# Clustered attention and two MLPs on one core: warming products read keys, the exponential's table is loaded early, the planner gets other durations, the second batch's values are read later

## The chip, the cores and the metric

The kernel runs on one core of a Trainium2 chip. The metric is the device time of one execution in microseconds (us). Engines are named as the profile names them: PE (TensorE, matrix products; PEld is its weight load), DVE (VectorE), ACT (ScalarE), POOL (GpSimd), SP (SyncE, which here issues every DMA).

## What is computed

Attention in which a query sees only the keys of its own cluster, then two MLPs in fp32 accuracy:

```
q_assign = argmax(q_n . c_n);  k_assign = argmax(k_n . c_n)      # 16 clusters per head, cosine
scores = where(q_assign == k_assign, q k^T / 8, -1e9)            # 2 batches, 8 heads, 768 x 768, head 64
attn = softmax(scores);  x = attn @ v                            # then (batch*seq, heads*64) = 1536 x 512
h = max(x @ w_in, 0);  x = (h * h) @ w_out                       # 512 -> 2048 -> 512
x = (sigmoid(x @ w_gate) * (x @ w_val)) @ w_out2                 # 512 -> 1536 -> 512
```

The MLP weights come as 64-bit floats and are turned into a high and a low fp32 part on the chip.

## The kernel before

**Attention.** Each of 16 heads has six score tiles of 128 queries by 768 keys, 96 in all, numbered n = 6 * head + i; tiles 2p and 2p+1 are pair p. For a tile PE makes the scores (`t_qk`) into one of two or three PSUM tiles `s`, DVE the negated maximum `nm` (`t_max`), ACT the exponential (`t_exp`) in place with a sum. Then ACT copies an fp16 high half into `hl` (`t_hi`) and DVE the low half (`t_lo`, L869). With both tiles of the pair done, one DMA transpose on SP makes `pt` from `hl` (`t_turn`, L878), and PE multiplies it with the values' halves `vh`, `vl` into `po` (`t_pv`). Pairs listed in `by_pe` go another way: the exponential is written to SBUF (`e`), PE transposes it (`tb`, L906), ACT or DVE copy it out (`ptf`), and the product with raw fp32 values follows. DVE scales `po` into `xp` (L961).

**A head's operands.** Raw queries and keys of two heads lie in one tile (`raw`, six buffers, loads on SP). Queries are scaled by 0.125 in place. For each head after the first, four tables T1, T2 (queries) and M1, M2 (keys) are built: a copy (`T<-raw`, `M<-raw`: ACT, DVE or POOL), a second copy (`T<-T`, `M<-M`: ACT, DVE, POOL, or a DMA), a subtraction (`T<-raw,T`, `M<-raw,M`: DVE or POOL), and rows of the one-hot assignment `oh` by DMA. The one-hot rows come from ten DVE steps on dots with the centroids (`as`), one set per four heads.

**The start** is written out by hand: 10 and 11 products that only keep PE at work (`keep_busy`), the dots, the first assignment, and `rt`, a square root on ACT.

**Order.** All else is put in order when the kernel is built, by `Planner`: a list scheduler with a duration per engine for each task (`{"a": 790, "p": 850}` lets ACT or POOL do it), a priority (mostly the tile's number less an offset out of `PLAN`), a time after which a result is seen (`SETTLE`), and counts of free buffers. DVE and POOL tasks marked `vp` are not put side by side. Each engine then runs its own list strictly in order. Weight conversions of the MLPs and the first third of the first MLP (`g`, `y` for 512 tokens) are put between the attention's work; the rest follows.

The second batch's values (`load_v`, six loads on SP, `vr`) may be issued from `v_later`, 50 us on the planner's clock.

```
def keep_busy(r, n):
    for _ in range(n):
        mm(busy[:, : r.shape[-1]], ident, r, True, True)
```

## Time and profile before

| | us |
|---|---|
| median of 3 runs (833.34 to 834.13) | 834.05 |
| profiled execution | 831.97 |
| its span | 830.2 |
| PE busy | 766.0 (92%) |
| DVE busy | 547.9 (66%) |
| ACT busy | 447.8 (54%) |
| POOL busy | 266.4 (32%) |

The shares are means over two different stages: up to about 360 us attention and MLP work run side by side, after it PE works through the MLPs alone. A busy share of the whole span therefore says little on what a change in the first stage is worth; the rows further down are taken by stretch. The span runs from the first instruction's start to the last one's end; the execution's own time has 1.8 us more.

### The profile page before, as it was taken

To read this page: it belongs to the slowest core of one execution; us is meant where nothing else is said; L and a number is where in the kernel's file an instruction comes from. 1 tells how busy PE (TensorE), PEld (TensorE's weight loads), DVE (VectorE), ACT (ScalarE), POOL (GpSimd) and SP (SyncE) were. 2 spreads that over 40 slices of the span, in tenths; PEclk is the share of its full clock that TensorE was granted. 3 is DMA by queue.
4 is the path that set the end of the run, shared out by engine and by line. 5 is a ranking of instruction groups with operands and counts; after the bars stand their busy time and mean duration, and the time that the engine had idled before them with its cause. 6 is when DMAs were issued, how large, how long until landed. Compare 5 with 4: busy or idle time off the path is not lost.

```text
span 830.2 us, 12473 instructions
## 1 busy us (share of the span) xinstructions
PE 766.0 (92%) x4721; PEld 633.7 (76%) x4721; DVE 547.9 (66%) x865; ACT 447.8 (54%) x800; POOL 266.4 (32%) x322
## 2 busy tenths in 40 slices
PE   8778687789888979799999999999999999999998
PEld 4468576668776868688888888888888888888886
DVE  5689888989999998868376776924333427933300
ACT  2989767778887675758564563422212225612300
POOL 3955646486555323334041322111111113100000
PEclk9889789999999989999999999999999999999999
DMA  6599997966889788732232322411211222100101
GB/s 201 137 191 211 181 191 158 214 130 137 165 207 212 180 194 185 268 102 95 83 127 76 102 80 98 135 68 54 98 51 51 76 78 102 51 24 27 39 26 38
DMA packets 143420, 100.56 MB, mean 121 GB/s; under 512 B 124128, under 2 KB 124128, under 8 KB 143360
## 3 DMA queue, kind: packets, MB, share of 16 engines
q1 hardware_dynamic: 143360, 99.76, 47.4%
q8 instruction: 37, 0.61, 0.3%
q14 instruction: 23, 0.19, 0.1%
HBM read 62.10 MB, written 3.15 MB: 79 GB/s over the span
## 4 chain that ended last, share of the span: by engine, by line
PE 68%; DVE 11%; DMA 8%; ACT 6%; issue 4%; POOL 1%; SPq 1%; DVEq 0%; POOLq 0%; ACTq 0%
PE y L310 14%; PE o L310 12%; PE pv L310 12%; PE pg L310 12%; PE g L310 11%; DMA pt<-hl 5%; DVE nm L839 3%; PE po L310 3%; PE s L310 3%; DMA wo0r<-in_moe_w_out_dram 2%; DVE hl L869 2%; ACT s L854 2%; ACT hl L317 2%; DMA raw<-in_k_dram 1%; DVE M L319 1%
## 5 line engine op out<-in xcount | busy, mean ns | idle before, releaser
L310 PE MATMUL s<-M,T 128*128 128x384 f32 x360 | 88.5, 375 | 28.2 <-DVE hl L869 14.2
L839 DVE TENSOR_REDUCE nm<-s 128x1 f32<-128x768 f32 x96 | 90.3, 950 | 10.6 <-PE s L310 9.9
L310 PEld LDWEIGHTS s<-M,T 128*128 128x128 f32 x360 | 65.2, 204 | 38.8 <-issue 14.1
L1442 DVE SCALAR_TENSOR_TENSOR gv<-th,pv 128x512 f32<-128x512 f32 x36 | 24.6, 687 | 98.2 <-PE pv L310 98.2
L1435 ACT ACTIVATE th<-pg 128x512 f32<-128x512 f32 x36 | 21.5, 598 | 123.9 <-PE pg L310 120.1
L854 ACT ACTIVATE s<-s,nm 128x768 f32<-128x768 f32 x78 | 68.1, 873 | 24.1 <-DVE nm L839 23.7
L869 DVE TENSOR_TENSOR hl<-s,hl 128x768 f16<-128x768 f32 x78 | 73.7, 948 | 4.0 <-ACT hl L317 3.6
L310 PEld LDWEIGHTS <-pt 128*128 128x128 f16 x1404 | 49.4, 104 | 24.0 <-DMA pt<-hl 13.8
L310 PE MATMUL po<-vh,pt 128*128 128x64 f16 x936 | 53.9, 202 | 13.8 <-DMA pt<-hl 9.1
L317 ACT ACTIVATE hl<-s 128x768 f16<-128x768 f32 x78 | 63.3, 811 | 1.9
L310 PE MATMUL po<-vl,pt 128*128 128x64 f16 x468 | 51.0, 202 | 0.0
L1471 ACT ACTIVATE ot<-o 128x512 f32<-128x512 f32 x12 | 7.2, 599 | 81.0 <-PE o L310 81.0
L1369 ACT ACTIVATE r<-g 128x512 f32<-128x512 f32 x48 | 28.7, 598 | 26.5 <-PE g L310 26.4
L1180 POOL TENSOR_SCALAR wgm<-wgm 128x512 f32<-128x512 f32 x12 | 7.7, 643 | 104.5 <-ACT wgm L1172 92.9
L1411 DVE TENSOR_TENSOR yf<-yf,y 128x512 f32<-128x512 f32 x36 | 24.7, 685 | 17.9 <-PE y L310 17.5
L776 POOL TENSOR_TENSOR T<-raw,T 64x768 fp32r<-64x768 f32 x15 | 29.3, 1954 | 4.1 <-ACT T L317 3.1
L782 POOL TENSOR_TENSOR M<-raw,M 64x768 fp32r<-64x768 f32 x15 | 28.3, 1887 | 1.4 <-DVE M L319 0.5
L1375 ACT ACTIVATE g<-r 128x512 f32<-128x512 f32 x47 | 28.3, 601 | 0.9
L1298 DVE TENSOR_TENSOR gs_0l<-gv,gs_0h 128x512 fp32r<-128x512 f32 x3 | 2.1, 690 | 39.3 <-ACT gs_0h L317 39.3
L1180 POOL TENSOR_SCALAR wi1m<-wi1m 128x512 f32<-128x512 f32 x16 | 10.4, 652 | 52.6 <-ACT wi1m L1172 45.6
L310 PEld LDWEIGHTS po<-vr,ptf 128*128 128x128 f32 x216 | 25.6, 192 | 0.2 <-DVE xp L961 0.2
L310 PE MATMUL po<-vr,ptf 128*128 128x64 f32 x216 | 25.6, 272 | 0.0
(583 smaller groups left out, 2359.5 us busy)
## 6 DMA issues: line engine op xcount, KB each, us to landing
wi0r<-in_moe_w_in_dram SPq DMA_DIRECT2D x16, 512.0 KB, 4.3
wo0r<-in_moe_w_out_dram SPq DMA_DIRECT2D x16, 512.0 KB, 4.0
wi1r<-in_moe_w_in_dram SPq DMA_DIRECT2D x16, 512.0 KB, 3.4
wo1r<-in_moe_w_out_dram SPq DMA_DIRECT2D x16, 512.0 KB, 3.3
wgr<-in_moe_w_gate_dram SPq DMA_DIRECT2D x12, 512.0 KB, 3.2
wvr<-in_moe_w_val_dram SPq DMA_DIRECT2D x12, 512.0 KB, 4.2
w2r<-in_moe_w_out_dram SPq DMA_DIRECT2D x12, 512.0 KB, 4.0
raw<-in_q_dram SPq DMA_DIRECT2D x8, 384.0 KB, 4.0
```

What stands on the lines that cost most here:

```text
L310: nc.tensor.matmul(o, lhsT=l, rhs=r, start=a, stop=z)
L317: nc.scalar.activation(out=out, in_=in_, func=AF.Copy, scale=scale)
L776: eng(e).tensor_tensor(out=T1[j][q], in0=raw[k][r], in1=T1[j][r].bitcast(F32), op=ALU.subtract)
L782: eng(e).tensor_tensor(out=M2[j][r], in0=raw[k][r], in1=M1[j][r].bitcast(F32), op=ALU.subtract)
L839: nc.vector.tensor_reduce(out=NM[n], in_=sc_ps[n][:, :, :HS], axis=AX.XY, op=ALU.max, negate=True)
L854: nc.scalar.activation(out=y, in_=x, func=AF.Exp, bias=NM[n], accum_out=SM[n // NQ][:, i : i + 1],)
L869: nc.vector.tensor_tensor(out=halves(hl[:, n % 2, 1]), in0=x[:, :, :HS], in1=halves(hl[:, n % 2, 0]), op=ALU.subtract,)
L1369: nc.scalar.activation(out=r, in_=banks["g1", c, f], func=AF.Relu)
L1375: nc.scalar.activation(out=p, in_=r, func=AF.Square)
L1411: nc.vector.tensor_tensor(out=yf[c, dm], in0=yf[c, dm], in1=p, op=ALU.add)
L1435: nc.scalar.activation(out=t, in_=p, func=AF.Tanh, scale=0.5)
L1442: nc.vector.scalar_tensor_tensor(out=o, in0=t, scalar=1.0, in1=p, op0=ALU.add, op1=ALU.mult)
```

## The change

- The 11 warming products behind the dots read a tile of keys (`raw[1, 0, 0]`) and no longer the queries.
- A tiny exponential on ACT (`warm`) stands right behind the square root, so that the table it needs is loaded there.
- The planner's table of numbers is another one. DMA tasks get longer durations (a transpose 3500 to 4600 ns, raw tiles 1092 to 1600, values 728 to 1100, weights 1456 to 2100) with a shorter `SETTLE` (2500 to 2100); POOL tasks get longer ones (a subtraction of 768 columns 1660 to 1880). PE and DVE are taken as free from 18.9 and 19.4 us on instead of 16.3 and 16.7.
- `v_later` goes from 50 to 100 us.
- `by_pe` has ten pairs (8 is out, 10 and 13 are in). A new list `by_pool` names tile 89: its exponential goes to SBUF and POOL makes its halves.
- Buffers of the stage slots are counted a little otherwise (`spare`, `xn`); `e_bufs` and `third` have the values that were fixed before.

```diff
-SETTLE = {"t": 200, "v": 120, "a": 130, "p": 130, "q": 2500}
+SETTLE = {"t": 200, "v": 120, "a": 130, "p": 130, "q": 2100}
...
-    "dup_q": 600, "exp": -2.2, "g_gate": 2, "g_split": -2.7, "group": 4, "h_gate": 5,
+    "dup_q": 700, "e_bufs": 2, "exp": 1.8, "g_gate": 2, "g_split": -4.7, "group": 4, "h_gate": 3,
...
-    "by_pe": (1, 7, 8, 16, 19, 24, 26, 30, 33,),
+    "by_pe": (1, 7, 10, 13, 16, 19, 24, 26, 30, 33,),
+    "by_pool": (89,),
...
-    plan = Planner({"t": 16300, "v": 16700, "a": 5600, "p": 6500, "q": 14100})
+    plan = Planner({"t": 18900, "v": 19400, "a": 5600, "p": 6500, "q": 14100})
...
     nc.scalar.activation(out=rt, in_=ss, func=AF.Sqrt)
+    warm = at.tile([P, 1], F32, name="warm")
+    nc.scalar.activation(out=warm, in_=rt, func=AF.Exp, scale=0.0)
...
-    keep_busy(raw[0, 0, 0][:, :HS], WARM[1])
+    keep_busy(raw[1, 0, 0][:, :HS], WARM[1])
...
-            add(qhi2, {"a": 790, "v": 469, "p": 850, "q": 750}, kind="dup", prio=pr + PLAN["build2"], after=[t0]),
+            add(qhi2, {"a": 790, "v": 469, "p": 900, "q": 900}, kind="dup", prio=pr + PLAN["build2"], after=[t0]),
             add(
-                qlo, {"v": 869, "p": 1660}, kind="qk_lo", prio=pr + PLAN["build2"], after=[t0],
+                qlo, {"v": 869, "p": 1880}, kind="qk_lo", prio=pr + PLAN["build2"], after=[t0],
...
     def t_hi(e, n):
         if n % 2 == 0:
             HL[n // 2] = tile_of("hl", (P, 2, 2, S), F16, f"hl{n}")
-        copy(e, halves(HL[n // 2][:, n % 2, 0]), sc_ps[n][:, :, :HS])
+        if n in by_pool:
+            copy(e, HL[n // 2][:, n % 2, 0], ET[n])
+        else:
+            copy(e, halves(HL[n // 2][:, n % 2, 0]), sc_ps[n][:, :, :HS])
...
-                lambda e, p=p: t_turn(e, p), {"q": 3500}, n - PLAN["turn"], after=[prev_lo, lo],
+                lambda e, p=p: t_turn(e, p), {"q": 4600}, n - PLAN["turn"], after=[prev_lo, lo],
```

Over the whole program this moves work between engines: of the second copies of keys and queries 12 went by DMA and now 2 do; ACT makes 27 first copies from raw instead of 17, DVE 3 instead of 13; DVE makes 7 of the subtractions, POOL 23 instead of 30; 38 pairs are transposed by DMA instead of 39.

**ACT at the start.** `jk` are passes over the values for their largest magnitude, `raw0_0_2` and `raw0_0_3` the third and fourth tile of queries (scaled in place), `s0` with `sm0` the first exponential. Before:

```order
L510 ACTIVATE jk0_5_32_269,am0_255<-vr0_5_11_135 128x512
L317 ACTIVATE M1_0_109<-raw1_0_1_5_122 64x768
L317 ACTIVATE raw0_0_2_12_137<-raw0_0_2_12_137 128x768
L854 ACT_TABLE_LOAD
L854 ACTIVATE s0_36_281,sm0_41_299<-s0_36_281,nm0_39_294 128x2x384
L317 ACTIVATE hl0_46_308<-s0_36_281 128x768
```

The same place on ACT after the change:

```order
L522 ACTIVATE jk0_5_32_270,am0_257<-vr0_5_11_135 128x512
L327 ACTIVATE M1_0_109<-raw1_0_1_5_122 64x768
L327 ACTIVATE raw0_0_2_12_137<-raw0_0_2_12_137 128x768
L327 ACTIVATE raw0_0_3_34_278<-raw0_0_3_34_278 128x768
L868 ACTIVATE s0_36_287,sm0_43_307<-s0_36_287,nm0_40_299 128x2x384
L327 ACTIVATE hl0_47_314<-s0_36_287 128x768
```

The table load has left this place (it now stands as ACT's third instruction, behind the square root), and the scaling of `raw0_0_3`, which POOL did before, stands ahead of the first exponential. The load of that tile on SP stands where it stood, behind two copies of the one-hot rows.

**PE at score tile 6**, the first of head 1 (`s6`, its two products with M1 and M2). Before:

```order
L906 MATMUL tb1_1_80_377<-ident_141,e2_63_349 128x128 x2
L906 MATMUL tb1_1_80_377<-ident_141,e3_69_359 128x128 x2
L310 MATMUL s6_83_384<-M1_1_110,T1_1_106 128x384 x2
L310 MATMUL s6_83_384<-M2_1_112,T2_1_108 128x384 x2
L906 MATMUL tb1_2_92_400<-ident_141,e3_69_359 128x128 x4
L310 MATMUL po1_95_407<-vr0_0_6_125,ptf1_72_361 128x64
```

The same place on PE after the change:

```order
L930 MATMUL tb1_1_80_380<-ident_141,e2_63_354 128x128 x2
L930 MATMUL tb1_1_80_380<-ident_141,e3_69_362 128x128 x2
L320 MATMUL s6_83_388<-M1_1_110,T1_1_106 128x384 x2
L320 MATMUL s6_83_388<-M2_1_112,T2_1_108 128x384 x2
L320 LDWEIGHTS pt0_59_347
L320 MATMUL po0_95_411<-vh0_0_329,pt0_59_347 128x64
```

The 36 products of pair 0 (`po0`), which wait for its transpose, have moved up from behind tile 9 to right behind tile 6.

**SP around the transposes of pairs 5 and 6** (`vr1` are the second batch's values). Before:

```order
L753 DMA M2_1_112<-oh0_246 16x768
L771 DMA M1_1_110<-M1_1_110 64x768
L334 DMA raw0_1_0_171_678<-in_q_dram 128x768
L334 DMA raw1_1_0_177_705<-in_k_dram 128x768
L878 DMA_TRANSPOSE pt5_181_732<-hl10_149_582 128x24x128
L340 DMA vr1_0_196_758<-in_v_dram 128x512
L878 DMA_TRANSPOSE pt6_199_767<-hl12_172_680 128x24x128
L771 DMA M1_0_109<-M1_0_109 64x768
L340 DMA vr1_1_222_852<-in_v_dram 128x512
```

The same place on SP after the change:

```order
L767 DMA M2_1_112<-oh0_248 16x768
L902 DMA_TRANSPOSE pt5_174_690<-hl10_150_605 128x24x128
L902 DMA_TRANSPOSE pt6_194_766<-hl12_170_677 128x24x128
L344 DMA raw0_1_0_214_839<-in_q_dram 128x768
L344 DMA raw1_1_0_222_856<-in_k_dram 128x768
L902 DMA_TRANSPOSE pt8_228_878<-hl16_210_830 128x24x128
```

The second copies of keys (`M1<-M1`) have left SP here, and the values' loads have moved to between the transposes of pairs 15 and 20.

## Rows read from the trace of the kernel before

**Rows 1.** By stretch: length, busy PE, PEld, DVE, ACT, POOL, clock, DMA.

```profile
26.00:160.00 134.00, 106.33 (x1103) 89.02 (x1102) 118.55 (x177) 109.16 (x203) 80.33 (x94) 0.88 0.92 181
160.00:325.00 165.00, 144.99 (x1306) 121.89 (x1306) 153.66 (x233) 124.61 (x222) 83.42 (x91) 0.96 0.82 180
...
360.00:830.00 470.00, 466.63 (x2059) 386.38 (x2057) 234.31 (x378) 184.18 (x321) 78.73 (x92) 1.00 0.21 73
```

**Rows 2.** Timeline of ACT at the start: start, duration, instruction, idle before, releaser.

```profile
18.21 0.84 ACT L317 ACTIVATE raw<-raw 128x768 f32<-128x768 f32 x1 [12.98 <-PE busy L310]
...
21.43 0.61 ACT L510 ACTIVATE jk<-vr 128x512 f32<-128x512 f32 x1
...
26.68 1.28 ACT L854 ACT_TABLE_LOAD   x1
27.97 0.88 ACT L854 ACTIVATE s<-s,nm 128x768 f32<-128x768 f32 x1
```

**Rows 3.** Timeline of DVE and SP at the start.

```profile
10.85 1.05 DVE L455 STREAM_TRANSPOSE d<-as 128x384 f32<-128x384 f32 x2 [4.14 <-PE as L310]
...
20.24 0.53 SPq L753 DMA_DIRECT2D M<-oh  x1
...
22.80 0.33 SPq L334 DMA_DIRECT2D raw<-in_q_dram  x1
...
25.23 0.16 DVE L515 TENSOR_REDUCE a<-am 128x1 f32<-128x6 f32 x1 [5.75 <-ACT jk L510]
```

**Rows 4.** Tile raw, 22.7 to 22.9 us: its load.

```profile
DMA to landing us min/median/max: 3.3/3.3/3.3
```

**Rows 5.** Timeline of POOL and DVE at 82 and 165 us.

```profile
81.73 1.82 POOL L776 TENSOR_TENSOR T<-raw,T 64x768 fp32r<-64x768 f32 x1
...
81.95 2.02 DVE L319 TENSOR_SCALAR M<-raw 64x768 fp32r<-64x768 f32 x1
...
165.22 0.54 DVE L319 TENSOR_SCALAR M<-raw 64x768 fp32r<-64x768 f32 x1
```

**Rows 6.** Timeline of SP and PE: the first transpose, score tile 6.

```profile
33.14 3.75 SPq L878 DMA_TRANSPOSE pt<-hl  x1
...
36.99 0.95 PE L310 MATMUL s<-M,T 128*128 128x384 f32 x4
```

**Rows 7.** Tile pt: landing, all 39, then the first alone.

```profile
DMA to landing us min/median/max: 5.5/6.1/8.4
...
DMA to landing us min/median/max: 7.2/7.2/7.2
```

**Rows 8.** Groups of DVE, 0 to 325 us: shapes, count, busy us, mean ns, idle.

```profile
L869 DVE TENSOR_TENSOR hl<-s,hl 128x768 f16<-128x768 f32 x78 | 73.7, 948 | 4.0 <-ACT hl L317 3.6
...
L319 DVE TENSOR_SCALAR M<-raw 64x768 fp32r<-64x768 f32 x8 | 7.8, 972 | 0.2
...
L319 DVE TENSOR_SCALAR M<-M 64x768 fp32r<-64x768 f32 x2 | 3.0, 1516 | 0.6 <-ACT M L317 0.6
...
L319 DVE TENSOR_SCALAR T<-raw 64x768 fp32r<-64x768 f32 x5 | 2.8, 559 | 0.1
L319 DVE TENSOR_SCALAR vh<-vr,sc 128x256 f16<-128x256 f32 x6 | 2.5, 439 | 0.0
```

**Rows 9.** Groups of PE, whole span.

```profile
L310 PE MATMUL po<-vh,pt 128*128 128x64 f16 x936 | 53.9, 202 | 13.8 <-DMA pt<-hl 9.1 <-DVE xp L961 3.7 <-DVE nm L839 1.0
...
L310 PE MATMUL po<-vr,ptf 128*128 128x64 f32 x216 | 25.6, 272 | 0.0
L906 PE MATMUL tb<-ident,e 128*128 128x128 f32 x108 | 17.6, 286 | 4.4 <-ACT e L854 1.8 <-ACT ptf L317 1.8 <-DVE a L525 0.7
```

**Rows 10.** Waits of PE: us in total, times, longest.

```profile
PE po L310 <- DMA pt<-hl: 9.1, 8, 3.5
...
PE s L310 <- ACT e L854: 4.5, 3, 2.2
```

**Rows 11.** Waits of DVE, 26 to 325 us.

```profile
DVE hl L869 <- ACT hl L317: 3.6, 9, 0.8
```

120 lines of the change are left out of this document (73 added, 47 removed).

## The prediction

> **What bounds the kernel now.** I read the busy time by stretch first, then the start in order of time, then the groups of instructions and the waits. The stretches say where TensorE sets the time [rows 1]: from 360 us to the end TensorE is busy for 466.6 of 470 us, with every weight ready. The change moves nothing there, so some 470 us of the span are fixed, and the change has the first 360 us to work on. There TensorE is busy for 106.3 of 134 us (26 to 160) and 145.0 of 165 (160 to 325), while VectorE is busy for 118.6 and 153.7, 88% and 93%. VectorE is thus the nearest thing to a bound of the attention, with TensorE next; the rest is waits that go round between scores, maxima, exponentials and halves. What the change is worth is the shift of the moment at which TensorE's solid stretch begins.
>
> The sums are made for the profiled execution, 831.97 us, of which 830.2 is span; the median of the three runs is 834.05, and I carry the difference found over to the median. About 0.2%, or 1.7 us, can be told from no change.
>
> **The start.** Today ScalarE stands still for 12.98 us until the warming products on TensorE end, because it scales in place the very queries that they read; only at 18.21 can it go on, and then come six passes over the values at 0.61 us (the first is shown, 21.43), a table load of 1.28 us and the first exponential at 27.97 [rows 2]. VectorE waits 5.75 us for those six passes [rows 3]. With keys as the operand the wait is gone: nothing writes that tile until its next load, which stands behind the products anyway. ScalarE can scale once the products of the cluster dots have ended, at 10.85 at the latest, when VectorE's first transpose has got them [rows 3]. Four copies of 0.84, six passes at 0.61 and two more copies end by 10.85 + 3.4 + 3.7 + 1.7 = 19.6 us. The table load is moved behind the square root, where ScalarE waits for queries: nothing.
>
> But the first exponential does not then start at 21. In the new order ScalarE scales one more query tile (raw0_0_3) just ahead of it; before, GpSimd did that one. This tile's load stands on SP behind two copies of the one-hot rows, the second of which is issued until 20.77 (20.24 + 0.53), since it waits for VectorE's assignment; today it is issued at 22.80 and lands 3.3 us later [rows 3, 4]. So: 20.8 + 3.3 + 0.84 = 24.9, exponential at about 25.1, 2.9 us earlier than today, not 7. Here the planner's own clock is wrong, since it starts SP at 14.1 us.
>
> Two things eat at the 2.9. First, GpSimd now works from about 10 us on, beside VectorE's ten steps of the assignment, while today it is idle there. What that can cost is seen later in the trace: a plain copy on VectorE takes 0.54 us at 165.22, and 2.02 at 81.95, where it lies under a GpSimd subtraction of 1.82 that began at 81.73 [rows 5]; so it waited 1.48. Four of the ten steps are of such a short form. Bounds: none, or two such waits, 3.0 us. (The Trainium skill, "GPSIMD Engine Reference", section Specifications, says that GpSimd shares its SBUF interfaces with VectorE, with contention for VectorE's two-port modes and for two SBUF inputs. That speaks against starting GpSimd early, and the pair of rows agrees; by that rule the start would lie nearer its bad end.) Second, in the new order TensorE's products of the first pair with values (po0) come right after score tile 6, before they came three tiles later. The pair's transpose takes 7.2 us from issue to landing, today from 33.14, and tile 6 ends at 37.94 [rows 6, 7]. With both moved by 2.9 the transpose lands at 37.4 and tile 6 ends at 35.0: TensorE stands for 2.4 us, and tile 7 keeps 0.5 of the 2.9. Bounds for the start: 2.9 gained if that wait is filled by what VectorE and ScalarE have queued, 2.5 lost if both mishaps come whole. I take 0.5 gained, between them, since the late tile 7 is the one that feeds VectorE next.
>
> (The Trainium skill, "ScalarE: Activation LUTs", section What ACT_TABLE_LOAD costs, gives 2.66 us for a switch, with the drain. The trace has 1.28 and the exponential 0.01 behind it; by the page the first exponential would gain 1.4 more, did it not wait for the query tile.)
>
> **VectorE's sum.** I count its instructions up to the last conversion of the first output weights, where the solid stretch begins, in the one order and the other, and price them [rows 8]. Copies of keys from raw: 8 to 1, -7 x 0.972 = -6.8. Copies of queries: 5 to 2, -1.7. Second copies of keys (M<-M): 2 to 5, +3 x 1.516 = +4.5. Subtractions that GpSimd did: +7; VectorE has none of this form, the nearest, with two tensors in and as many columns, are the low halves of scores, 0.948, so +6.6. Low halves of scores: 78 to 75 (one more pair through TensorE, one tile through GpSimd), -3 x 0.948 = -2.8. Value copies -3 x 0.439 = -1.3. One more one-hot step and the weights' low halves: +0.5. Together -1.0. The mean of M<-M is of two; at the 0.948 of the other forms the sum is -2.7, and at 2.08, the rest of that mean, it is +0.7. I take -1.8, between the first two, as the planner now gives GpSimd's subtractions 1.88 us, and [rows 5] shows 1.82, so it will put a copy under one less often. Since VectorE is 88 to 93% busy there, this counts nearly whole.
>
> **Transposes and loads.** TensorE waits 9.1 us in all, 8 times, for transposes to land [rows 10]. They take 6.1 us in the median, 8.4 at most [rows 7]; the planner reckoned with 3.5 + 2.5 = 6.0 and now with 4.6 + 2.1 = 6.7. That takes up to 0.7 from each of eight waits, 5.6. Ten copies through DMA fewer, and the six loads of the second batch's values out from among the transposes of pairs 5 to 9, push the same way. But VectorE, not TensorE, is the fuller engine: I take 2.0 gained, bounds 0 and 5.6. The values' loads themselves are off the path in both orders: the first product with the second batch's values is past tile 48, and the loads stand on SP by pair 15 to 18.
>
> **TensorE's own work.** Ten pairs go through TensorE instead of nine. By the groups of [rows 9] a pair's transposes take 17.6 / 9 = 1.96 us and its products 25.6 / 9 = 2.84, where a DMA pair's products take 53.9 / 39 = 1.38: +3.4 us. What covers them is TensorE's idle time, 27.7 us between 26 and 160, where the pair lies; I take nothing, and 3.4 if that cover is gone.
>
> **ScalarE** gets ten more copies of 0.84 us (7 of keys, 3 of queries), and some halves of weights. It is busy for 234 of 299 us between 26 and 325 [rows 1]; taken at nothing here, the rival below prices it. GpSimd gets less; tile 89's halves are in its slack.
>
> Sum: -0.5 - 1.8 - 2.0 = -4.3, so 831.97 goes to 827.7, and the median to **829.8 us**.
>
> **Rivals.**
> Slower: ScalarE's queue. Each added copy stands in order ahead of exponentials and halves. VectorE now waits 3.6 us for ScalarE's halves, TensorE 4.5 for exponentials [rows 10, 11], which speaks against it; 78% busy, and the end of GpSimd's and DMA's help with these copies, speak for it. If half of the 8.4 us lands on the path, 4.2, and the extra pair's 3.4 with it, while VectorE's lighter sum turns into idle time, the time is 834.05 - 0.5 - 2.0 + 7.6 = 839; with half of that price, 836. It decides from the point where the two waits together grow by more than the 4.3 that I count as gain.
> No change: the early GpSimd work slows the assignment and po0 stands at the head of TensorE's queue (start lost by about 1.5), VectorE's sum gains only 1.0: 834.05 + 1.5 - 1.0 - 0.5 for transposes = 834. This is also the case in which the change doesn't do what it says: the table is early, the exponential is not.
> Faster by more: the start keeps all of 2.9, VectorE 2.7, transposes 5.6: 823. For it speaks that TensorE's longest single wait for a transpose is 3.5 us [rows 10], so that few of them make up most of the 9.1.
>
> **How the numbers follow.** Forecast 0.44, faster by more 0.16, no change 0.17, slower 0.23. Faster by over 0.2% is then 0.60, within 0.2% 0.17, slower 0.23. The range goes from 821, a little past the sum of the good bounds, to 838, inside the slower rival, and leaves out under 0.2.
>
> **What would show it.** The first exponential at 25 us (22 or 27.5 would show a misread queue or the slowed assignment); ScalarE's longest wait at the start for a query load, not for TensorE; a wait of TensorE for a transpose at 35 to 38 us; VectorE's busy time to 325 down by 1 to 3 us; TensorE's waits for transposes below 6 us; the solid stretch from about 354 us. The forecast is wrong if waits of VectorE and TensorE for ScalarE double, or if TensorE's idle time before 360 us falls by far more than 8 us.

## The result and the profile after

The changed kernel takes 838.46 us in the median of 13 runs (834.08 to 843.0), the kernel before beside it 832.65 (13 runs). The ratio is 1.0075, 95% interval 1.005 to 1.0101: **slower, by 6.2 us** (5.8 between the two medians), where I had forecast 829.8 and "faster". Below, a ratio is always against the kernel before on the same chip in the same hour; 0.001 of it is 0.83 us.

The profiled execution of the changed kernel is its fastest of the 13 (834.08 us, span 832.3), while that of before (831.97) is near its median. So the trace shows some 2 us of the loss; the rest is in no trace of this kernel, and only experiments and the clock of the other runs can say something about it.

By stretch (columns as in [rows 1]: length, busy PE, PEld, DVE, ACT, POOL, clock, DMA share, GB/s). The start, which [rows 1] leave out, in the kernel before:

```profile
0.00:26.00 26.00, 17.35 (x65) 10.76 (x66) 11.48 (x30) 10.06 (x21) 11.93 (x34) 0.95 0.56 179
```

After the change, from the start on:

```profile
0.00:26.00 26.00, 20.12 (x65) 11.55 (x66) 15.49 (x30) 12.20 (x23) 18.88 (x37) 0.90 0.51 162
26.00:160.00 134.00, 103.44 (x1110) 87.82 (x1108) 118.01 (x175) 112.52 (x212) 75.00 (x96) 0.93 0.85 174
160.00:325.00 165.00, 146.83 (x1304) 124.52 (x1305) 152.34 (x225) 126.40 (x227) 75.80 (x86) 0.94 0.82 171
...
360.00:830.00 470.00, 468.50 (x2067) 387.64 (x2066) 234.45 (x384) 185.68 (x325) 73.26 (x87) 1.00 0.22 74
```

VectorE's work between 26 and 325 us fell from 272.2 to 270.4 us, about what its sum of instructions had said; but in the first 26 us it rose by 4.0 (11.48 to 15.49), so that up to 325 us it is some 2 us more than before. ScalarE's, between 26 and 325 us, rose from 233.8 to 238.9. The last stretch is full, as before.

The start, on DVE: the five assignment steps that got longer, and the first maximum (start, duration, instruction, idle before, releaser).

```profile
14.66 0.98 DVE L483 TENSOR_TENSOR w<-eq,rank 128x768 f16<-128x768 f16 x1
...
16.67 1.47 DVE L494 TENSOR_TENSOR eq<-w,m 128x768 f16<-128x768 f16 x1
...
19.26 1.84 DVE L571 TENSOR_SCALAR TM<-ot 16x768 f32<-16x768 f16 x1
21.11 1.09 DVE L329 TENSOR_SCALAR TM<-ot 16x768 f32<-16x768 f16 x1
22.24 2.04 DVE L510 TENSOR_SCALAR oh<-ot,aux_a,aux_b 128x768 f32<-128x768 f16 x1
...
25.40 0.96 DVE L853 TENSOR_REDUCE nm<-s 128x1 f32<-128x768 f32 x1 [1.05 <-PE s L320]
```

Two of GpSimd's instructions beside them; the first, a copy, overlaps the `eq<-d,mx` that comes before these five steps:

```profile
13.60 1.65 POOL L331 TENSOR_SCALAR M<-M 64x768 fp32r<-64x768 f32 x1
...
18.89 1.79 POOL L790 TENSOR_TENSOR T<-raw,T 64x768 fp32r<-64x768 f32 x1
```

The same place on SP and ACT:

```profile
25.04 0.53 SPq L767 DMA_DIRECT2D M<-oh  x1
25.75 0.45 SPq L344 DMA_DIRECT2D raw<-in_q_dram  x1
...
29.10 0.84 ACT L327 ACTIVATE raw<-raw 128x768 f32<-128x768 f32 x1 [11.98 <-DMA raw<-in_q_dram]
29.85 0.86 ACT L868 ACTIVATE s<-s,nm 128x768 f32<-128x768 f32 x1
```

The first exponential's maximum is there at 26.36, but ScalarE stands for the fourth query tile's load, which stands on SP behind the one-hot rows, which stand behind the slowed assignment. It starts at 29.85, 1.9 us later than in [rows 2] and 4.7 later than I had forecast.

Waits (us in total, times, longest) of PE from 26 to 360 us and of DVE from 26 to 325. Two of the kernel before that [rows 10, 11] leave out:

```profile
PE s L310 <- DVE hl L869: 14.9, 18, 1.6
...
DVE nm L839 <- PE s L310: 9.9, 11, 2.5
```

And after the change:

```profile
PE s L320 <- DVE hl L893: 20.9, 17, 3.1
PE po L320 <- DMA pt<-hl: 7.3, 5, 2.8
PE tb L930 <- ACT ptf L327: 5.6, 4, 2.9
...
PE s L320 <- ACT e L868: 1.1, 2, 0.8
...
DVE nm L853 <- PE s L320: 13.7, 23, 1.2
DVE hl L893 <- ACT hl L327: 5.9, 9, 2.7
```

TensorE's waits for transposes fell from 9.1 [rows 10] to 7.3 and those for exponentials from 4.5 to 1.1, but its waits for a score buffer (VectorE's low halves) rose from 14.9 to 20.9, those for ScalarE's copies of transposes from 1.8 [rows 9] to 5.6, and VectorE's for scores from 9.9 to 13.7. The table moved waits about: TensorE's idle time from 26 to 360 us is 54.2 us, where it was 52.0.

**Behind the last exponential** lies the whole loss of this trace. The 96th exponential starts at 321.02 us here and at 322.13 in the kernel before, so the attention itself is 1.1 us early; from there to the end of the span it takes 511.3 us and not 508.1. The first 45 us of that stretch, with the sum over all of it and two waits of TensorE, before the change:

```profile
322.13:367.13 45.00, 40.72 (x250) 33.83 (x249) 36.52 (x62) 27.69 (x49) 16.30 (x20) 0.96 0.63 200
...
sum 508.07, PE 500.23 PEld 414.29 DVE 266.84 ACT 206.36 POOL 92.28; mean PE 250.11 PEld 207.14 DVE 133.42 ACT 103.18 POOL 46.14
...
344.10 1.89 PE L1090 MATMUL xq<-ident,xp 128*128 128x128 f32 x8 [3.50 <-DVE g_15l L1276]
...
350.34 0.50 PE L310 MATMUL y<-g_12h,wo0h 128*128 128x512 f32 x1 [0.78 <-DVE yf L1411]
```

and after it (the waits are TensorE's longest and its last; here one wait is both):

```profile
321.02:366.02 45.00, 39.56 (x241) 32.75 (x240) 37.78 (x65) 26.49 (x47) 13.97 (x16) 0.92 0.62 195
...
sum 511.27, PE 502.04 PEld 415.42 DVE 267.97 ACT 209.18 POOL 85.49; mean PE 251.02 PEld 207.71 DVE 133.99 ACT 104.59 POOL 42.74
...
346.50 1.12 PE L1120 MATMUL xq<-ident,xp 128*128 128x128 f32 x4 [4.70 <-DVE x_0l L1310]
```

TensorE is idle 1.4 us longer and busy 1.8 us longer, in a stretch in which its clock is lower (0.92 against 0.96). It stands 4.70 us for a low half (`x_0l`) that VectorE makes only behind conversions of the MLP's weights; in the kernel before its longest wait there is 3.50 us.

### The profile page after: what moved, and what is told of

Read it like the earlier page. It is cut to its first block, busy times and chain, and to the rows that moved or that the text cites. A ratio compares the mean times of both kernels' runs of the same rounds, so it can differ in the third digit from the quotient of the medians.

```text
span 832.3 us, 12437 instructions
## 1 busy us (share of the span) xinstructions
PE 768.4 (92%) x4721; PEld 636.1 (76%) x4721; DVE 550.4 (66%) x863; ACT 457.4 (55%) x823; POOL 253.3 (30%) x316
## 4 chain that ended last, share of the span: by engine, by line
PE 58%; DVE 0%; ACT 0%; issue 0%
PE y L320 12%; PE o L320 12%; PE pg L320 12%; PE pv L320 12%; PE g L320 10%; PE xq L1120 0%; DVE x_0l L1310 0%; DVE wo0l L1279 0%; ACT ot L1506 0%
## 5 line engine op out<-in xcount | busy, mean ns | idle before, releaser
L320 PE MATMUL s<-M,T 128*128 128x384 f32 x360 | 87.1, 374 | 25.1 <-DVE hl L893 20.4
L853 DVE TENSOR_REDUCE nm<-s 128x1 f32<-128x768 f32 x96 | 89.7, 949 | 14.0 <-PE s L320 13.7
L868 ACT ACTIVATE s<-s,nm 128x768 f32<-128x768 f32 x75 | 65.3, 870 | 27.4 <-DVE nm L853 27.0
L893 DVE TENSOR_TENSOR hl<-s,hl 128x768 f16<-128x768 f32 x75 | 70.5, 948 | 6.0 <-ACT hl L327 5.9
L320 PE MATMUL po<-vh,pt 128*128 128x64 f16 x912 | 51.8, 202 | 9.8 <-DMA pt<-hl 7.3
L327 ACT ACTIVATE hl<-s 128x768 f16<-128x768 f32 x75 | 59.8, 808 | 0.9
L320 PE MATMUL po<-vl,pt 128*128 128x64 f16 x456 | 49.0, 201 | 0.0
L1446 DVE TENSOR_TENSOR yf<-yf,y 128x512 f32<-128x512 f32 x36 | 24.6, 684 | 15.9 <-PE y L320 15.6
L320 PE MATMUL po<-vr,ptf 128*128 128x64 f32 x240 | 29.0, 273 | 1.6 <-ACT ptf L327 0.8
L320 PEld LDWEIGHTS po<-vr,ptf 128*128 128x128 f32 x240 | 28.8, 192 | 2.1 <-DVE xp L985 1.2
L1214 POOL TENSOR_SCALAR wi1m<-wi1m 128x512 f32<-128x512 f32 x16 | 11.5, 720 | 57.4 <-ACT wi1m L1206 47.5
L930 PE MATMUL tb<-ident,e 128*128 128x128 f32 x120 | 19.5, 285 | 8.6 <-ACT ptf L327 5.6
L796 POOL TENSOR_TENSOR M<-raw,M 64x768 fp32r<-64x768 f32 x13 | 24.9, 1913 | 3.7 <-ACT M L327 2.8
L1279 POOL TENSOR_TENSOR wvl<-wvm,wvh 128x512 fp32r<-128x512 f32 x9 | 11.6, 1290 | 43.6 <-ACT wvh L327 43.6
```

The source lines that it names most:

```text
L320: nc.tensor.matmul(o, lhsT=l, rhs=r, start=a, stop=z)
L327: nc.scalar.activation(out=out, in_=in_, func=AF.Copy, scale=scale)
L796: eng(e).tensor_tensor(out=M2[j][r], in0=raw[k][r], in1=M1[j][r].bitcast(F32), op=ALU.subtract)
L853: nc.vector.tensor_reduce(out=NM[n], in_=sc_ps[n][:, :, :HS], axis=AX.XY, op=ALU.max, negate=True)
L868: nc.scalar.activation(out=y, in_=x, func=AF.Exp, bias=NM[n], accum_out=SM[n // NQ][:, i : i + 1],)
L893: nc.vector.tensor_tensor(out=halves(hl[:, n % 2, 1]), in0=x[:, :, :HS], in1=halves(hl[:, n % 2, 0]), op=ALU.subtract,)
```

## The experiments

All times are medians, with the ratio and its interval. The second table shows how far each kernel is on its way: the start, on ScalarE, of the nth exponential of its profiled execution, and in the last column the time from the 96th, the last, to the end of the span. In the labels, b_ stands for the kernel before and a_ for the changed one.

| | median us | ratio | interval |
|---|---|---|---|
| after | 838.46 | 1.0075 | 1.0050 to 1.0101 |
| b_start | 829.55 | 0.9978 | 0.9956 to 1.0001 |
| a_plan_only | 836.97 | 1.0085 | 1.0046 to 1.0123 |
| a_scale_pool | 835.96 | 1.0049 | 1.0022 to 1.0076 |
| a_hold | 838.12 | 1.0070 | 1.0048 to 1.0092 |
| b_hold | 831.23 | 0.9992 | 0.9967 to 1.0018 |
| a_hold2 | 838.65 | 1.0071 | 1.0039 to 1.0103 |
| b_hold_d | 825.87 | 0.9929 | 0.9903 to 0.9955 |
| b_start_d | 828.64 | 0.9980 | 0.9957 to 1.0004 |
| a_all | 834.70 | 1.0047 | 1.0025 to 1.0068 |
| a_thin | 835.20 | 1.0038 | 1.0013 to 1.0064 |
| b_thin | 832.77 | 0.9996 | 0.9969 to 1.0023 |
| a_vthin | 836.24 | 1.0071 | 1.0042 to 1.0100 |
| a_pairs | 838.88 | 1.0093 | 1.0067 to 1.0119 |
| a_v50 | 847.42 | 1.0184 | 1.0157 to 1.0211 |
| a_oldtab | 851.69 | 1.0241 | 1.0214 to 1.0267 |
| b_newtab | 827.09 | 0.9954 | 0.9930 to 0.9977 |
| a_olddma | 831.33 | 0.9984 | 0.9957 to 1.0012 |
| nt_hold_d | 829.62 | 0.9969 | 0.9943 to 0.9995 |

| exponential | 1st | 10th | 40th | 43rd | 94th | 96th | 96th to end |
|---|---|---|---|---|---|---|---|
| before | 28.0 | 46.0 | 126.3 | 135.0 | 311.1 | 322.1 | 508.1 |
| after | 29.9 | 48.9 | 120.8 | 135.4 | 309.9 | 321.0 | 511.3 |
| b_start | 27.8 | 46.2 | 124.1 | 132.8 | 305.8 | 316.9 | 508.1 |
| a_plan_only | 29.7 | 50.1 | 121.9 | 136.6 | 311.1 | 322.2 | 511.2 |
| a_scale_pool | 26.4 | 46.0 | 120.0 | 137.3 | 312.5 | 324.4 | 509.9 |
| a_hold | 28.9 | 48.0 | 122.0 | 139.3 | 315.6 | 326.9 | 511.2 |
| b_hold | 22.3 | 45.7 | 126.5 | 135.9 | 313.4 | 323.6 | 509.1 |
| a_hold2 | 21.6 | 47.5 | 119.8 | 134.5 | 309.0 | 320.1 | 511.2 |
| b_hold_d | 21.9 | 40.5 | 120.8 | 127.1 | 303.5 | 314.2 | 509.7 |
| a_all | 22.2 | 41.9 | 116.4 | 133.8 | 310.0 | 321.3 | 511.3 |
| a_v50 | 30.0 | 48.6 | 127.1 | 131.2 | 315.1 | 321.0 | 520.8 |
| a_oldtab | 28.1 | 47.3 | 131.9 | 137.8 | 315.3 | 323.0 | 523.7 |
| b_newtab | 27.5 | 48.7 | 126.7 | 131.1 | 308.8 | 319.9 | 505.2 |
| a_olddma | 26.7 | 46.1 | 121.8 | 128.5 | 308.4 | 319.6 | 509.9 |

### The start alone, the plan alone

In b_start:

```diff
-    nc.scalar.activation(out=rt, in_=ss, func=AF.Sqrt)
+    nc.scalar.activation(out=rt, in_=ss, func=AF.Sqrt); warm = at.tile([P, 1], F32, name="warm"); nc.scalar.activation(out=warm, in_=rt, func=AF.Exp, scale=0.0)
...
-    keep_busy(raw[0, 0, 0][:, :HS], WARM[1])
+    keep_busy(raw[1, 0, 0][:, :HS], WARM[1])
```

and a_plan_only is the changed kernel with the same edits undone.

> The kernel before, with the two edits of the start alone: the warming products read keys, and the tiny exponential stands behind the square root. Its plan, and with it the order on every engine, stays. Theory A (the start is what made the change slower): GpSimd's copies and subtractions again run beside VectorE's ten assignment steps and lengthen them from 8.6 to about 12.7 us; but GpSimd scales the fourth query tile here, so ScalarE waits only for the first maximum and the first exponential comes at 26 to 27.5 us, not at 29.85; the time is 831 to 832, or 838 if what hurts is the early GpSimd work as such. Theory B (the new plan between 26 and 325 us made it slower, by ScalarE's queue or by waits of VectorE and TensorE): 830.5 to 833 us, about the kernel before less the earlier exponential.

> The changed kernel with both edits of the start undone: the products read queries again, and there is no early exponential, so that the table is loaded ahead of the first one. The new plan stays, and the order on every engine with it. The assignment should take 8.6 us again; the fourth query tile's load is issued at about 22.8, lands at 26.1 and is scaled by ScalarE, and with the table load the first exponential comes at about 28.3 us, 1.5 earlier than in the changed kernel and as in the one before. Theory A (the start): 832.5 to 834.5. Theory B (the plan): 836.5 to 838.5, since what comes after the start is the same.

The two start edits don't hurt the old order (0.9978; by its interval little gain or none), and the new order without them is as slow as with them (1.0085 against 1.0075). So the loss sits in the plan, its start included. One expectation was off: a_plan_only's assignment took 8.6 us again, but its first exponential still came at 29.7, since ScalarE there goes on only at 19.22, when the products end. That run thus doesn't tell the plan's start from the plan behind it.

### What stops the first exponential

a_scale_pool moves one task to GpSimd; a_hold makes GpSimd wait for the assignment.

```diff
-                lambda e, k=kq: copy(e, raw[k], raw[k], 0.125), {"a": 790, "p": 900}, pr - 0.5,
+                lambda e, k=kq: copy("p" if k == (0, 0, 3) else e, raw[k], raw[k], 0.125), {"a": 790, "p": 900}, pr - 0.5,
```

```diff
-    assign_end(0)
+    assign_end(0); held = at.tile([1, 1], F32, name="held"); nc.gpsimd.tensor_scalar(out=held, in0=OH[0][0:1, 0:1], scalar1=1.0, scalar2=0.0, op0=ALU.mult, op1=ALU.add)
```

> The changed kernel with one task moved: the scaling of the fourth query tile (raw0_0_3) is made by GpSimd, where it stands idle from 24 to 33 us, and no longer by ScalarE ahead of the first exponential. ScalarE's wait of 12 us for that tile's load should go, and the first exponential come when its maximum is there, at 26.4 us, 3.4 earlier. Theory A: the end comes earlier by as much, 834.5 to 835.5. Theory B: what is gained at the start is lost again in the first 100 us, where VectorE and TensorE wait for each other; 837 to 838.5.

> The changed kernel with one tiny GpSimd instruction more, which reads one element of the first one-hot tile and stands ahead of GpSimd's first copy: GpSimd does not start on head 0's and 1's tables until VectorE has ended the assignment. If the overlap with GpSimd is what lengthened the assignment, it takes 8.6 us again (12.75 in the changed kernel), the load behind the one-hot rows is issued at about 21.7, and the first exponential comes at about 26, 3.9 earlier. But GpSimd's eight instructions come some 10 us later, and end at about 34 instead of 24, which may delay score tile 6 (38.85) and the values' low halves behind them. Theory A: 834.5 to 836. Theory B: 837.5 to 839. If GpSimd's later tables set the end: 840 and more.

a_scale_pool: first exponential at 26.4, as reckoned; 1.0049, some 2.2 us less than the changed kernel, though the intervals overlap. a_hold shows what GpSimd did to the assignment; the same steps on DVE with GpSimd held:

```profile
15.70 0.56 DVE L483 TENSOR_TENSOR w<-eq,rank 128x768 f16<-128x768 f16 x1
...
17.28 0.96 DVE L494 TENSOR_TENSOR eq<-w,m 128x768 f16<-128x768 f16 x1
...
19.36 0.55 DVE L571 TENSOR_SCALAR TM<-ot 16x768 f32<-16x768 f16 x1
19.92 0.55 DVE L329 TENSOR_SCALAR TM<-ot 16x768 f32<-16x768 f16 x1
20.51 0.68 DVE L510 TENSOR_SCALAR oh<-ot,aux_a,aux_b 128x768 f32<-128x768 f16 x1
```

Against the changed kernel these five are shorter by 0.42, 0.51, 1.29, 0.54 and 1.36, 4.1 us together, which is the whole difference of the assignment (12.75 to 8.63). But the kernel is no faster (1.0070): held there, GpSimd was also late with the second query tile, for which ScalarE stood 11.49 us, and the first exponential came only at 28.9.

### The start set free

b_hold and a_hold2 hold GpSimd one instruction later, behind its scaling of the second query tile; a_hold2 also has the edit of a_scale_pool.

> The kernel before with both edits of the start, and GpSimd held back: right behind its scaling of the second query tile it has one tiny instruction that reads one element of the first one-hot tile, so that its copies and subtractions for heads 1 and 2 begin when VectorE has ended the assignment, as they did before. All else keeps its place in the order. If GpSimd beside VectorE is what lengthens the assignment, it takes 8.6 us again (11.9 with the start edits alone), the first score tile's maximum needs no longer wait, and the first exponential comes at 23.5 to 25 us instead of 27.8. Theory A (what the start gives goes through to the end): 825.5 to 827. Theory B (the middle of the attention takes it back): 829 to 830.5.

> The changed kernel with GpSimd held back in the same way, behind its scaling of the second query tile (which ScalarE waits for), and with the scaling of the fourth query tile on GpSimd and no longer on ScalarE. Both losses of its start should be gone: assignment 8.6 us, first exponential at 23.5 to 25 us (29.85 in the changed kernel, 26.4 with the scaling moved alone). Theory A (the start): 5 us off the changed kernel's 838.3, 832.5 to 834. Theory B (the plan behind it): 835 to 837, no better than with the scaling moved alone.

In both the first exponential came some 6 us earlier than in the kernel before (22.3 and 21.6), and in both next to nothing of it was left at the tenth exponential (45.7 and 47.5, against 46.0 there). Neither is faster than its parent; for a_hold2 both of the expected ranges were too low. What took it back stands in the traces. In b_hold, DVE and POOL at 40 us:

```profile
40.10 0.19 DVE L953 RECIPROCAL d<-d 128x6 f32<-128x6 f32 x1 [5.63 <-POOL d L945]
...
39.80 0.27 POOL L945 TENSOR_SCALAR d<-sm,sc 128x2 f32<-128x2 f32 x1
```

In a_hold2, PE:

```profile
37.37 0.23 PE L320 MATMUL po<-vh,pt 128*128 128x64 f16 x1 [5.77 <-DMA pt<-hl]
```

VectorE stood for head 0's softmax sums, three tiny GpSimd operations queued behind its work on the values, with a low half behind it in order. TensorE stood for pair 0's transpose, whose products the new plan puts right behind score tile 6: the wait that my prediction had named, 2.2 us long in the changed kernel itself, and 5.8 as soon as the start is early.

So in b_hold_d and b_start_d VectorE makes those sums:

```diff
-            nc.gpsimd.tensor_scalar(
+            (nc.gpsimd if hd else nc.vector).tensor_scalar(
                 out=DN[hd][:, i:k], in0=x[:, i:k], scalar1=1e-9, ...
```

> The kernel before with both edits of the start, GpSimd held until the assignment has ended, and one thing more: head 0's three tiny operations for the softmax sums (d) are made by VectorE, right ahead of the reciprocal that uses them, and no longer by GpSimd, where they stand behind twelve operations on the values. With GpSimd held alone, the first exponential came at 22.3 us, 5.7 earlier than before, and all of it was gone at score tile 9 (45.7 us), after VectorE had stood 5.63 us at that reciprocal. Theory C1 (this wait alone took the lead back): tile 9's exponential at 40 to 42 us and an end 4 to 5 us earlier, 826 to 827.5. Theory C2 (behind it stands the next wait, for the first transposes or for GpSimd's low halves of the values): tile 9 at 43 to 46 us, and 829 to 831.5.

> The kernel before with both edits of the start and head 0's softmax sums on VectorE, but with GpSimd not held: what is left of the version of 825.9 us when GpSimd may work beside the assignment. Theory L (GpSimd beside VectorE is what cost the start its gain): assignment 12 us, first exponential at 27 to 28 us, 829 to 831. Theory M (the wait for GpSimd's sums alone was the point): 825.5 to 827.5, whatever the first exponential does.

**b_hold_d is 825.87 us, ratio 0.9929, faster than both kernels.** Its lead is 6.1 us at the first exponential, 5.5 at the tenth and 7.6 at the 94th: in the old order, once that wait is gone, the start goes through to the end (the span is 6.3 us shorter). Without the hold (b_start_d) the first exponential comes at 26.7 and the ratio is 0.9980; hold and sums are worth something only together.

a_all does the same to the changed kernel and puts pair 0's products behind those of pair 1 (three helpers call back later; the planner's list stays).

> The changed kernel with its start set free as far as in the kernel before that was fastest so far: GpSimd held until the assignment has ended, the fourth query tile scaled by GpSimd, head 0's softmax sums (d) made by VectorE, and the products of pair 0 with the values put behind those of pair 1, where the kernel before has them; before that, TensorE stood 5.77 us for pair 0's transpose at score tile 7. The rest of the order is the new plan's. Theory N1 (the new plan's loss lies behind the start and stays): the first exponential at 22 and tile 9's at 41 us, 8 us earlier than in the changed kernel, and the end 6 earlier, 831 to 833.5. Theory N2 (the new plan was hurt at its start alone): 825 to 828. Theory N3 (the lead is lost again between 60 and 150 us, to TensorE's waits and the lower clock that goes with them): 835 to 838.

1.0047: 2.3 us less than the changed kernel (the intervals overlap), with its first exponential 7.6 and its tenth 7.0 us earlier. The lead is 4.4 us at the 40th, 1.6 at the 43rd and nothing at the 94th. Theory N3 comes nearest: the middle of the new plan takes the start back, so by these two runs, a_scale_pool and a_all, the start explains about 2 us of the 6.2.

### Between the 40th and the 43rd exponential

Kernels with the new order take long here: after needs 14.7 us from the 40th to the 43rd, before 8.8. In the trace of after this only gives back a lead: it is 5.5 us ahead of before at the 40th, 0.4 behind at the 43rd, and 1.1 ahead again at the last. In a_scale_pool, two windows there (columns as in [rows 1]), and from the timelines TensorE's wait and what ScalarE then waits for:

```profile
120.50:127.50 7.00, 4.11 (x66) 3.71 (x65) 6.94 (x10) 6.41 (x14) 3.45 (x5) 0.99 0.87 191
127.50:137.60 10.10, 9.72 (x64) 9.56 (x61) 5.66 (x12) 3.92 (x10) 2.64 (x2) 0.50 0.99 211
```

```profile
126.68 0.66 PE L930 MATMUL tb<-ident,e 128*128 128x128 f32 x4 [2.89 <-ACT ptf L327]
...
137.27 0.88 ACT L868 ACTIVATE s<-s,nm 128x768 f32<-128x768 f32 x1 [5.56 <-DVE nm L853]
```

TensorE works 4.11 of 7 us, standing 2.89 for ScalarE's copy of a transpose; right behind that the granted clock is 0.50, so 1.2 GHz and no longer 2.4, for 10 us in which TensorE is busy for 9.72, and the next score tiles come late. The same wait (2.88, 2.89, 2.61) stands at the same place in a_all, after and a_vthin; in a_all the clock of 123 to 131 us is 0.54, in after that of 127.4 to 134 is 0.79 and that of 141 to 148 is 0.50. What follows the wait thus differs from one profiled execution to the next, and the time with it: in after, a_plan_only and a_hold2 the 40th to the 43rd take 14.7 us, in a_scale_pool, a_hold, a_all, a_thin and a_vthin, with the same order on TensorE there, 17.2 to 17.4. The kernel before has stretches at a lower clock too (0.78 from 100 to 120 us), and over the whole span its profiled execution has a granted clock of 0.968, that of after 0.969.

Is it ScalarE's queue that makes the wait? a_thin and b_thin cut ScalarE's first copies of keys and queries, a_vthin its passes over the second batch's values:

```diff
-            copy(e, T1[j][r], raw[k][r])
+            w = 64 if e == "a" and (k[1] or 2 * k[2] + j > 2) else S; copy(e, T1[j][r][:, :w], raw[k][r][:, :w])
...
-            copy(e, M1[j][r], raw[k][r])
+            w = 64 if e == "a" and (k[1] or 2 * k[2] + j > 2) else S; copy(e, M1[j][r][:, :w], raw[k][r][:, :w])
```

```diff
-        nc.scalar.activation(out=jk, in_=V[b, t], func=AF.Abs, accum_out=vst[b][:, t : t + 1])
+        c = 8 if b else DM; nc.scalar.activation(out=jk[:, :c], in_=V[b, t][:, :c], func=AF.Abs, accum_out=vst[b][:, t : t + 1])
```

> The changed kernel with 23 of ScalarE's copies of keys and queries cut from 768 to 64 columns, from head 3 on; the rest of those tables is left as it was, so that scores come from partly stale operands. Place and order of every instruction stay. That takes about 23 x 0.65 = 15 us of work from ScalarE. Theory B1 (ScalarE's queue is the new plan's cost: halves, exponentials and copies of transposes wait behind these copies): TensorE's waits for ScalarE's copies of transposes (5.6 us) and VectorE's for its halves (5.9) fall by more than half, and the time by 4 us or more, to 834 or less. Theory B2 (the places of the pairs on TensorE and the clock that follows from its waits): 836.5 to 838.5.

> The kernel before with its own 13 such copies cut in the same way (8.5 us less for ScalarE), with the same stale operands. It tells what such a cut is worth where ScalarE's queue is not what the plan pays for. Theory B1: 0 to 1.5 us less than the kernel before, clearly less than the same cut gives in the changed kernel per copy. Theory B2: the gain per copy is the same in both.

> The changed kernel in which ScalarE's six passes over the second batch's values read 8 of 512 columns, so that the scale of these values comes from those alone; place and order of every instruction stay. It takes 6 x 0.45 = 2.7 us from ScalarE between 119 and 131 us, where TensorE waits 2.9 us for a copy of a transpose that stands behind one of these passes. Theory S (ScalarE's queue is what stops TensorE there, and the half clock that follows it makes it dear): that wait falls below 2 us, tile 42's exponential comes 2 to 4 us earlier against tile 39's, and the time is 834.5 to 836.5. Theory T (TensorE's own order there, with three pairs' products ahead of tile 42, sets it): 837 to 839.

a_thin gained about 3 us on the changed kernel (1.0038), b_thin nothing (0.9996). That is in favour of ScalarE's queue; but the waits that should have fallen by half did not (TensorE for copies of transposes 5.4 us, VectorE for halves 6.2, against 5.6 and 5.9), and the intervals of a_thin and after overlap. a_vthin is at 1.0071, and its wait at that place is still 2.61. So what these runs show of ScalarE's queue is 3 us at most for the copies that a_thin cut, and by which wait is not shown.

### Pairs, values, durations, table

Here the planner makes a new order from other numbers.

> The changed kernel with the old nine pairs for TensorE (8 in, 10 and 13 out) and no tile for GpSimd; all other numbers of the table are the new ones, and the order is planned anew with them. Theory F (the tenth pair and its place cost the plan its time: a pair through TensorE takes 3.4 us more there, and its transposes wait for ScalarE's copies): 833.5 to 835.5. Theory G (offsets and durations do it, whichever pairs they order): 836.5 to 839.

> The changed kernel with the second batch's values read from 50 us on the planner's clock again, planned anew. Theory V (the late values push their six passes on ScalarE, and the scale that hangs on them, into the stretch from 119 to 140 us, where the changed kernel loses 6 us on the kernel before): 833 to 835.5, and tile 42's exponential no longer 14 us behind tile 39's. Theory G: 836.5 to 839, with the same loss between tiles 39 and 42.

> The changed kernel with the planner's old table: the old offsets, the old nine pairs, no tile for GpSimd, values from 50 us on. What stays of the change are the two edits of the start, the new durations and settling times, the planner's later clock for TensorE and VectorE, and the counting of buffers. Theory D (the new durations make the order that is slower): 836 to 839. Theory E (the new table of offsets and pairs makes it): 829 to 832, as the kernel before with the two edits of the start (829.6).

> The kernel before with both edits of the start and the new table (offsets, ten pairs, values from 100 us on; GpSimd's tile 89 is left out, since this kernel has no code for it), but with the planner's old durations, settling times and clocks. It is the fourth corner of a square: old table with old durations 829.6, new table with new durations 838.3, old table with new durations 851.5. Theory D1 (the new durations do harm by themselves, some 20 us, and the new table makes good what it can): 826 to 831 us. Theory D2 (table and durations are fitted to each other, and either one changed alone gives a worse order): 837 us and more.

> The changed kernel with the planner's old numbers for DMA alone (transposes 3500, raw tiles 1092, values 728, weights 1456, second copies 750, seen 2500 later); GpSimd's new durations, the later clocks of TensorE and VectorE, tile 89, the counting of buffers and the new table stay. The old durations all together gave 827.0 with the new table, the new ones 838.3. Theory Q1 (the longer DMA durations make the worse order, since SP's list is planned as if it were full and tasks are put off): 826 to 831. Theory Q2 (GpSimd's durations and the later clocks, which move copies from GpSimd and DMA to ScalarE and put tasks behind each other at the start, make it): 835 to 840. Between: both halves.

a_pairs (the old nine pairs, no tile for GpSimd) gives 1.0093: the tenth pair isn't the cause, as far as a new order can tell. a_v50 (values from 50 us again) gives 1.0184, worse by 9 us: one number of the table, changed alone, moves the result by more than the whole change did, so undoing numbers one by one doesn't share out the loss. Neither of the theories' ranges held there, nor in a_oldtab. The square does it better:

| | old durations | new durations |
|---|---|---|
| old table, start edits | 0.9978 (b_start) | 1.0241 (a_oldtab) |
| new table, start edits | 0.9954 (b_newtab) | 1.0075 (after) |

The new table is good: under the old durations it may gain a little (0.9954 against 0.9978, intervals overlapping), and under the new ones it makes good 14 of 22 us. **The new durations do the harm**, 10 us under the new table and 22 under the old one. (The right column also has the later clocks of TensorE and VectorE, the other counting of buffers and, in after, tile 89.) In the profiled executions most of this lies behind the last exponential. From b_newtab to after the last exponential comes 1.1 us later, and the rest takes 6.1 us longer; from b_start to a_oldtab it is 6.0 and 15.6; and a_v50 has its last exponential where after has it, with 9.5 us more behind it. There TensorE is busy for 510.4 us in a_v50 and 502.0 in after, so more of its work is left for the end.

a_olddma goes back with the DMA numbers alone:

```diff
-SETTLE = {"t": 200, "v": 120, "a": 130, "p": 130, "q": 2100}
+SETTLE = {"t": 200, "v": 120, "a": 130, "p": 130, "q": 2500}
...
-                lambda e, p=p: t_turn(e, p), {"q": 4600}, n - PLAN["turn"], after=[prev_lo, lo],
+                lambda e, p=p: t_turn(e, p), {"q": 3500}, n - PLAN["turn"], after=[prev_lo, lo],
```

(also raw tiles 1600 to 1092, values 1100 to 728, weights 2100 to 1456, second copies 900 to 750.) That gives 0.9984, 7.6 us of the 10, near Theory Q1. (As a_v50 warns, any such edit makes another order: a_olddma shows that the old DMA numbers give one without the loss, not why.) And TensorE's waits between 26 and 360 us in a_olddma show that it isn't by fewer waits for transposes:

```profile
PE po L320 <- DMA pt<-hl: 15.9, 12, 3.9
PE s L320 <- DVE hl L893: 14.6, 18, 3.5
```

It waits 15.9 us for transposes, twice as long as the changed kernel (7.3), and is 7.6 us faster. Its waits for score buffers are back at 14.6; but that isn't the answer either, since b_newtab, faster still, waits as long for them as the changed kernel (20.9):

```profile
PE s L312 <- DVE hl L871: 20.7, 20, 2.3
```

Three things differ besides. Its first exponential comes at 26.7 and not at 29.9, for there GpSimd scales the fourth query tile. Behind the last exponential it takes 509.9 us and not 511.3. And over the runs its granted clock is 0.9725 in the mean (12 runs; the kernel before beside it 0.971, on the other chips 0.973 to 0.974), that of after 0.963 (13 runs). Within the 13 runs of after a run is 4.1 us shorter for each 0.01 of clock, and 2.5 to 6.1 us within those of nearly every other kernel. By that, 0.01 goes with some 4 us, and with the 2.2 of a_scale_pool for the start this comes to about the 6.2. It is an estimate made after the event: that the lower clock costs the time is not shown, since fewer waits could give both the higher clock and the shorter time, and no run here held the clock fixed.

The last run puts the two edits that free the start on b_newtab.

> The kernel before with both edits of the start and the new table under the old durations (827.0), and with the two edits that freed the start: GpSimd held until the assignment has ended, and head 0's softmax sums on VectorE. In the old table these two gave 4 us more (829.8 to 825.7). Theory C1 (the lead of the start goes through to the end in this order too): first exponential at 22 us, tile 9's at 42 to 44 instead of 48.7, 822 to 824. Theory C2 (a later wait takes it back, as in the changed kernel with its start freed, where 8 us at the start became 3.5 at the end): 824.5 to 827.

It gains nothing on b_newtab (0.9969 against 0.9954), and both expected ranges were too low. Its first exponential is at 21.7 us, its tenth at 49.2, no earlier than b_newtab's; between them ScalarE stands for a load of weights, and TensorE for ScalarE:

```profile
33.25 0.66 ACT L1174 ACTIVATE wi0m<-wi0r 128x512 f32<-128x512 f32 x1 [2.57 <-DMA wi0r<-in_moe_w_in_dram]
34.66 0.66 ACT L1174 ACTIVATE wi0m<-wi0r 128x512 f32<-128x512 f32 x1 [0.75 <-DMA wi0r<-in_moe_w_in_dram]
...
35.85 1.11 PE L908 MATMUL tb<-ident,e 128*128 128x128 f32 x4 [3.81 <-ACT ptf L319]
```

## Why the prediction was wrong, step by step

**What the change is worth.** I took the last 470 us as fixed ("the change moves nothing there") and the shift of the moment at which TensorE's solid stretch begins as all there is to gain. In the trace TensorE's last wait ends 3.8 us earlier than before (346.50 against 350.34), and the span ends 2.1 us later: with another order other work is left behind the attention, and 3.2 us are lost there. For that step no term stood in my sum.

**The start.** The chain was right: assignment, one-hot rows, load of the fourth query tile, its scaling, first exponential. The mis-sized term is the price of GpSimd's early work, bounded at 0 to 3.0 us as two waits of short copies and measured at 4.1, on five steps, one of them (`eq`) of a form that I had not counted. With 0.7 us for products that began later (11.53 against 10.85 [rows 3]) the forecast of 25.1 becomes 29.9, as seen. I took 0.5 us gained; 1.9 were lost at the first exponential and 2.9 at the tenth. The Trainium skill, "SBUF — State Buffer", section Who interferes with whom, says that VectorE and GpSimd hold a shared pair of ports one at a time for a whole instruction, where VectorE's has two SBUF inputs or runs in a two-port mode, but not for a reduction; the trace agrees (`w`, the second `eq`, TM and `oh` stretched, the two reductions stayed at 0.95).

**What the start is worth.** I carried the first exponential's shift over to the end one to one. b_hold and a_hold2 show that to be wrong: 6 us were gone by the tenth exponential, at the next queue that was late anyway. The po0 wait that I named was real, but it is one of several such seconds.

**VectorE's sum.** Forecast -1.8, and between 26 and 325 us it is -1.8 (272.2 to 270.4). That is in part luck: the second copies of keys cost +1.1 us and not +4.5, the subtractions +7.9 and not +6.6, and the assignment's second `eq` took +1.4 more, which I had not counted. And by my own sign, the busy time up to 325 us, it rose by some 2 us, for the start added 4.0. The failed step is "counts nearly whole". VectorE's waits for scores and halves rose by 6.1 us (9.9 + 3.6 to 13.7 + 5.9), so less work for it gave no time back.

**Transposes.** Right as a wait: -2.0 forecast, -1.8 measured (9.1 to 7.3). The failed step is that fewer waits for transposes are a gain: a_olddma has twice as many and is faster.

**TensorE's tenth pair** at nothing: right, as far as a_pairs shows.

**ScalarE's copies at nothing**, and the slower rival: that rival's time (839; with half its price its own terms give 835.4, not 836) is what came out, and a_thin gives it up to 3 us. But its mechanism is not shown, so that this agreement may be luck. By its own test (VectorE's waits for halves and TensorE's for exponentials growing by more than 4.3 together) it failed: they went from 8.1 to 7.0. The waits that grew are those for score buffers and for copies of transposes.

**What I didn't weigh at all** is the planner's new view of DMA. I had used the longer numbers only to ask when a transpose is seen. They also fill SP's list in the planner's eyes: 38 transposes at 1.1 us more and 32 loads of weights at 0.64 more are 62 us, nearly all of it in the first 325. Nor are they truer than the old ones. From issue to landing a transpose takes 6.1 us in [rows 7] and 6.3 here,

```profile
pt<-hl SPq DMA_TRANSPOSE x38, 6.3
```

between the old numbers (3.5 + 2.5 = 6.0) and the new (4.6 + 2.1 = 6.7). And to the planner the first of these terms is the time for which SP can issue nothing else. In the trace that is shorter (ns, least, median and most):

```profile
L902 SPq DMA_TRANSPOSE pt<-hl x38: 3530/3743/5291, 34.7 to 323.9; - x38
...
L1196 SPq DMA_DIRECT2D wi0r<-in_moe_w_in_dram x16: 328/371/583, 27.9 to 322.4; - x16
```

So 3.5 was near the 3.74 of a transpose and 4.6 is not, and for a load of weights both numbers (1.46 and 2.1) are far above 0.37. The transfers overlap: from issue to landing the 111 DMAs between 26 and 325 us of the changed kernel add up to 515 us in a stretch of 299. That the DMA numbers make the difference, a_olddma shows; that it is by a list planned as too full is argued, not shown. Nor did I reckon with the clock, which by the estimate above goes with the larger part of the loss.

## What to carry to other kernels

A list scheduler's durations and its offsets are one fitted set, and a duration has to mean in the model what was measured: a queue's time to landing is not the time for which it is taken. Here the old DMA numbers alone took back 7.6 us. An earlier first step is worth only as much as the next late queue allows, so look up, before costing it, what else is queued for the same moment; here the gain came when the third such wait was removed. And a shorter wait on one row of the table is no gain until the waits beside it, and those behind the stage, are added up: in the trace the stage that I had studied ended early, and the loss stood behind it.

## What had not been expected of the hardware

- VectorE and GpSimd hold each other up in both directions: beside GpSimd's copies and subtractions the copy `TM` took 1.84 us for 0.55 and `oh` 2.04 for 0.68; GpSimd's own copy `M<-M` took 1.65 for 0.83 in the same stretch. Reductions (0.95) and transposes (0.98) of VectorE were not touched.
- The start of the assignment differed between the profiled executions, from 10.85 us (before) to 12.56 (a_hold), with the landing of the first key loads: TensorE's last four products for it wait for one until 9.34 and 11.05.
- The same wait of 2.9 us on TensorE was followed by 10 us at half its clock in a_scale_pool (0.50), but by 0.79 over the next 6.6 us in after. Within the 13 runs of after the mean clock of an execution goes with its time, 4.1 us shorter for 0.01 more.
